# The third token group of batch 0 gets its second product as seven block products

## The chip, the cores and the metric

The kernel runs on one core of one Trainium2 chip. TensorE (PE in the profile) multiplies matrices, with weight loads shown as a unit of their own (PEld); VectorE (DVE), ScalarE (ACT) and GpSimd (POOL) work element by element; the SP queue and the POOL queue issue the DMAs. The metric is the device time of one execution in microseconds (us). The kernel before takes 362.45 us, the median of 3 runs (362.01 to 362.58).

## The reference

Attention over 4 batches of 768 tokens with 8 heads of 64, each token seeing 4 sink tokens and a window of 128, and behind it a dense mixture of 4 experts over the 3072 tokens:

```python
keep = is_sink | in_window
a = softmax(where(keep, scale * q @ k.T, -1e9))
x = (a @ v)                       # per batch [768, 8 * 64], together [3072, 512]
p = domain_probs / (domain_probs.sum(-1, keepdims=True) + 1e-09)
for e in range(E):                # 4 experts, w1 [512, 1024], w2 [1024, 512]
    h = np.maximum(x @ w1[e], 0.0)
    out += p[:, e:e + 1] * (h @ w2[e])
```

## The kernel before, in words

Tokens are taken in groups of 256; (b, g) is group g (0 to 2) of batch b (0 to 3). For each group and each expert e there is a *unit* (b, g, e): its first product `x @ w1[e]` with ReLU, kept in a tile H. There are at most 6 tiles H at a time (`NH = 6`); three more come free near the end.

**First products.** A *slow* unit is 32 products of 256 columns (line 1055). A *fast* unit multiplies 2 by 2 blocks with seven block products (`UNITS`, names P1 to P7), 56 products of 128 columns (line 1142), for which DVE forms sums of tokens (line 1111) and, once per expert, sums of the weights (`weight_form1`, lines 374 to 380), and for which ACT and DVE copy and add partial blocks (lines 1188, 1195, 1201, 1210). `START[e]` is the first (b, g) from which expert e is fast.

**Second products, batch 0.** Batch 0 has plain second products (`emit_second`): for each unit and each half s of the group 8 products of 512 columns (line 1394), then one DVE instruction that multiplies by the token's gate and adds to the output tile (lines 1404 and 1406). ReLU of batch 0 is done without the gate, on ACT or DVE, whichever is free (lines 1068, 1070, 1161, 1163). Each output half is stored through SP (line 1412).

**Second products, batches 1 to 3.** Here the gate is multiplied in with the ReLU, on DVE alone (`scalar_tensor_tensor`, lines 1079 and 1175), and the second product of a group is seven block products in the order `CHAIN = ("P1", "P2", "P6", "P5", "P7", "P3", "P4")` (`emit_product`). Since the gate is already in H, all four experts are summed in one PSUM bank: each block product is 4 experts times 4 products of 256 columns (line 1316). DVE forms four sums per unit of H for it (`chore`, lines 1260 and 1239) in two tiles S, and three or four sums of w2 per expert (`weight_form`, lines 338 to 344). A block's result goes out by a copy on ACT (line 1366; P1 also seeds the other bank, line 1348) or an addition on DVE (lines 1354 and 1359). `PAIRS` lists the groups done so: nine, all of batches 1 to 3. A tile H is held until its part of P4, the last.

Three facts tie batch 0 to the first of these groups. The tiles S lie in the buffers of the outputs of batch 0's groups 0 and 1, so that the sums of the first pair wait until these are stored. The sums of w2 of expert 3 lie in three buffers (`spare_rows`) that are left over once the six q and k tiles of batch 1 have been turned by DMA transposes on SP (line 243). And no block product is emitted while a plain second product is still due (`product_ready`).

**Order.** Everything is in one program order that a planner in the kernel writes: it keeps a modelled clock per engine, and at each step takes, among the instructions of TensorE that are ready, the one with the lowest priority number (attention steps, first products, block products, plain second products). Evictions wait in a list with a slack each (`GATE`, `MASK`, `FORM`, `TOKEN`), and go to ACT or DVE by it. If nothing is ready, it issues products of zeros (line 554). The constants at the top (lines 60 to 90) set priorities, slacks and the points at which the attention of the next batch begins (`LEAD`, in parts of the work done). The loads that POOL issues have a fixed order: after the attention of batch 0 it asks for w1 of expert 3, then for the rows of q, k and v of batch 1, and then for w2 of expert 3 (line 319). The gates per token are written to DRAM (line 438) and read back as one broadcast tile per unit (line 454), five at a time.

Of the kernel before, what the change touches and what calls it, by code (L numbers as in the profile page):

```python
# [16 lines left out]
def kernel(  # L17
# [14 lines left out]
    B, H, S, D = q.shape  # L32
    NSINK = int(n_sink)
    WIN = int(window)
    E, Dm, F = moe_w1.shape
    Ntok, Dout = out.shape

    P = 128
# [8 lines left out]
    NDB = Dm // P  # L47
    NFB = F // P
# [3 lines left out]
    G = 2 * P  # L52
    NG = S // G
# [6 lines left out]
    NGATE = 5  # L60
    START = {0: (0, 2), 1: (0, 2), 2: (0, 0), 3: (2, 1)}
    MIX = 4
    SHARE_OF = (0.98, 0.90, 1.01)
    LEAD = (0.92, 0.94)
    DUE = 0
    LOW_PRODUCT = 2.005
    LOW_SECOND = 2.7
    HIGH_PRODUCT = 1
    EARLY = 0.01
    MASK = 2500  # L70
    GATE = 3000
    GATE0 = 500
    FORM = 9000
    TOKEN = 5000
    MARGIN = 1000
    HOLD = 0
    FULL = 7
    STEP0 = 0.3
    READY = 40
    WIDE = 2  # L80
    OPEN = 2.6
    SOON = 21000
    ROWS1 = 1500
    ONACT = 1
    ONE = 2
    PAIR = 1
    BEHIND = 1500
    CHORES = 2
    OWN = 2
    BIASED = 1  # L90
    FAST = tuple(START)
# [292 lines left out]
    used, formed = set(), {}  # L384
    left = [NG] * E

# [54 lines left out]
    gate_sb = {}  # L441
# [474 lines left out]
    QF = NFB // 2  # L916
    PAIRS = [(b, g) for b in range(1, B) for g in range(NG)]
    CHAIN = ("P1", "P2", "P6", "P5", "P7", "P3", "P4")
# [3 lines left out]
    class Mixture:  # L922


        def __init__(self):
            self.early = {g: list(range(E)) for g in range(NG)}
            self.open = []
            self.units = []
            for b, g in PAIRS:
                fast = [e for e in range(E) if self.is_fast(b, g, e)]  # L930
                slow = [e for e in range(E) if e not in fast]
                while fast or slow:
                    for x in (fast, slow):
                        if x:
                            self.units.append((b, g, x.pop(0)))
# [28 lines left out]
        def opened(self, b, g, e):  # L964
# [9 lines left out]
            def complete(at):  # L974
                self.H_at[b, g, e] = at
                self.finished.add((b, g, e))
                if b:
                    self.waiting.append((b, g, e))
                    load_gates()
# [20 lines left out]
        def firsts(self):  # L1000

            early = sum(map(len, self.early.values()))
            zero = sum(u["unit"][0] == 0 for u in self.open)
            n = len(self.open)
# [8 lines left out]
            if n < WIDE and early:  # L1013
                at, g = self.next_early()
                yield at, (OPEN if n else 2), ("early", g)
            if n < WIDE and self.units and early <= MIX and self.room() and not (early + zero and self.live >= NH - 1):
                yield self.unit_ready(*self.units[0], False), (OPEN if n else 2) - EARLY, ("unit",)

        def emit_first(self, what, ready):
# [15 lines left out]
            b, g, e = u["unit"]  # L1035
            if j in (0, "P1") and (b, e) == (0, E - 1) and not gate_sb:
                load_gates()
            u["left"].remove(j)
            if not u["left"]:
                self.open.remove(u)  # L1040
                left1[e] -= 1
                if b == 0:
                    self.second += [(g, s, e) for s in range(2)]
# [20 lines left out]
            part = self.H_part[b, g, e]  # L1064
            if b == 0:
                def run(engine):
# [20 lines left out]
        def tokens(self):  # L1087

            pairs = [x for x in [(0, g) for g in range(NG)] + PAIRS if any(self.is_fast(*x, e) for e in FAST)]
            n = len(self.T)  # L1090
# [28 lines left out]
        def emit_fast(self, u, m, ready):  # L1119
# [37 lines left out]
            def gated(dst, src, half_, ready, slack, slot=None, then=None):  # L1157
                if b == 0:
                    def relu(engine):
# [59 lines left out]
        def chore(self):  # L1219
# [25 lines left out]
            if any(x[:2] < (b, g) and x[2] == "P5" for x in self.products) or any(x[:2] < (b, g) for x in self.last):  # L1245
                return False
            if (b, g) == PAIRS[0] and (len(self.stored) < 2 * NG or self.stored[-1] > t["pe"] + 500):
                return False
# [30 lines left out]
        def product_ready(self):  # L1279
# [8 lines left out]
            if m == "P1" and self.piece == E - 1 and acc_free[1 - bank] > 1e11:  # L1288
                at = 1e12
            if self.second or any(u["unit"][0] == 0 for u in self.open) or any(self.early.values()):  # L1290
                return 1e12
# [135 lines left out]
    att = Attention(0)  # L1427
    work = [E * NG * 2 * NFB * NDB * G - sum(mix.is_fast(0, g, e) for g in range(NG) for e in FAST) * NFB * P] + [NG * E * NFB * G * (NDB + 7 / 4) - sum(mix.is_fast(b, g, e) for g in range(NG) for e in FAST) * NFB * P for b in range(1, B)]
    ahead, upto, loaded, wide = 0, 0.0, 0, 0
# [22 lines left out]
    while mix.more() or att.more():  # L1452
# [5 lines left out]
        if not att.more() and not loaded:  # L1458
            loaded = 1
            gates_by_row()  # L1460
            turns += [(1, tb) for tb in range(NQB)]
            loads.append((load_w1, 3))
            for tb in range(NQB):
                loads.append((load_nat, 1, tb))
                if tb % 2:
                    loads += [(load_v, 1, (tb - 1,)), (load_v, 1, (tb,))]
            loads.append((load_w2, 3))
        x = next((x for x in loads if load_ready(x) < now + 1500), None)
# [39 lines left out]
        if soonest > 1e11:  # L1508
            if loads:
                x = loads.pop(0)  # L1510
                x[0](*x[1:])
            else:
                turn_nat(*turns.pop(0))
            continue
# [46 lines left out]
```

## Time and profile before

| | |
|---|---|
| median of 3 runs | 362.45 us |
| the profiled execution | 362.36 us, span 360.7 us |
| granted TensorE clock, mean | 0.999 |
| PE busy | 354.0 us (98%) |
| DVE busy | 299.2 us (83%) |
| ACT busy | 165.6 us (46%) |
| POOL busy | 71.3 us (20%) |
| line 1394, plain second products | 192 products |
| line 1316, block products | 1008 products |
| line 1142, fast first products | 2072 products |
| line 1055, slow first products | 352 products |

An engine's busy time is the time in which at least one of its instructions runs. For PE the ends are modelled, and products overlap: the row of line 1394 gives 379 ns for one, but eight in a row start 216 ns apart. The pace (starts of neighbours, or the length of a long run divided by its number) is what a product costs. The times run from the start of the span; the profiled execution took 1.7 us more than its span.

### The profile page before, as it was taken

The page shows a single profiled execution, that of the slowest core. Times are in us where ns is not written, and L with a number is a line of the kernel's source. Part 1 is how long each engine was busy: PE and PEld are TensorE (multiplying, and loading weights), DVE is VectorE, ACT ScalarE, POOL GpSimd, SP SyncE. Part 2 cuts the span into 40 slices and gives each one's busy share as a digit, 9 for nine tenths or more (in the row PEclk, how much of TensorE's full clock was granted, in tenths as well). Part 3 has the DMA queues.
Part 4 walks back from the last instruction along what each step waited for, and adds up shares of the span by engine and source line. Part 5 has one row for each costly group of instructions (what it writes and reads, how often), then busy time and mean ns, then how long its engine had stood idle before and what let it go on. Part 6 is the DMA issues. An engine that isn't in the chain of part 4 may idle for free.

```text
span 360.7 us, 10596 instructions
## 1 busy us (share of the span) xinstructions
PE 354.0 (98%) x4436; PEld 297.8 (83%) x4436; DVE 299.2 (83%) x671; ACT 165.6 (46%) x419; POOL 71.3 (20%) x92
## 2 busy tenths in 40 slices
PE   8899999999999999999999999999999999999996
PEld 3585767766668878898899899899999999999985
DVE  6775989896588989789879989969999898897850
ACT  5764734479483475464454365544213312213210
POOL 8936116400624307010610000000000000000000
PEclk9999999999999999999999999999999999999999
DMA  9999999999998999528998212122011011100011
GB/s 165 167 183 193 211 210 163 127 148 214 164 96 146 162 199 128 72 49 97 137 168 127 60 64 53 19 75 61 22 54 59 25 52 47 31 33 29 2 59 58
DMA packets 117291, 37.25 MB, mean 103 GB/s; under 512 B 100612, under 2 KB 112740, under 8 KB 117244
## 3 DMA queue, kind: packets, MB, share of 16 engines
q0 software_dynamic: 77520, 17.31, 54.4%
q1 hardware_dynamic: 38668, 18.75, 26.6%
q8 instruction: 34, 0.56, 0.6%
q10 hardware_dynamic: 1056, 0.52, 0.5%
q14 instruction: 13, 0.11, 0.1%
HBM read 40.45 MB, written 6.34 MB: 130 GB/s over the span
## 4 chain that ended last, share of the span: by engine, by line
PE 88%; DVE 6%; ACT 2%; DMA 1%; issue 1%; POOL 1%; ACTq 0%; DVEq 0%
PE cps L1142 31%; PE acc L1316 29%; PE acc L1394 11%; PE hps L1055 10%; PE od L747 3%; PE sps L681 3%; DVE H L1175 2%; DMA vx<-in_v_dram 1%; ACT aT L706 1%; PE od L740 1%; DVE S L1260 1%; PE tx L805 1%; DVE onat L777 1%; DVE H L1210 1%; DVE osb L1404 0%
## 5 line engine op out<-in xcount | busy, mean ns | idle before, releaser
L1142 PEld LDWEIGHTS <-w 128*128 128x128 bf16 x1184 | 73.6, 98 | 4.2 <-issue 1.3
L1316 PEld LDWEIGHTS <-H 128*128 128x128 bf16 x600 | 56.1, 98 | 6.1 <-issue 0.5
L706 ACT ACTIVATE aT<-sps 128x512 bf16<-128x512 f32 (+1 forms) x96 | 47.0, 571 | 16.2 <-PE sps L681 16.1
L1175 DVE SCALAR_TENSOR_TENSOR H<-cps,gates 128x512 bf16<-128x512 f32 x78 | 52.5, 681 | 0.8
L1142 PEld LDWEIGHTS <-vf 128*128 128x128 bf16 x768 | 47.0, 98 | 1.9 <-issue 0.3
L1316 PE MATMUL acc<-w,H 128*128 128x256 bf16 x360 | 47.5, 273 | 0.0
L1394 PE MATMUL acc<-w,H 128*128 128x512 bf16 x192 | 45.3, 379 | 0.0
L1142 PE MATMUL cps<-T,w 128*128 128x128 bf16 x592 | 45.0, 219 | 0.1
L1142 PE MATMUL cps<-xT,w 128*128 128x128 bf16 x592 | 44.7, 219 | 0.0
L1055 PE MATMUL hps<-xT,w 128*128 128x256 bf16 x352 | 43.6, 273 | 0.0
L786 ACT ACTIVATE onat<-od,R 128x64 bf16<-128x64 f32 x144 | 33.0, 330 | 19.2 <-DVE R L774 18.7
L1188 ACT COPY cps<-cps 128x512 f32<-128x512 f32 x37 | 21.4, 578 | 41.6 <-PE cps L1142 38.0
L1142 PE MATMUL cps<-T,vf 128*128 128x128 bf16 x512 | 37.4, 219 | 0.0
L1055 PEld LDWEIGHTS <-w 128*128 128x128 bf16 x352 | 33.0, 98 | 4.5 <-issue 0.6
L1394 PEld LDWEIGHTS <-H 128*128 128x128 bf16 x192 | 17.7, 98 | 18.1 <-issue 0.5
L296 POOL DMA_DIRECT2D vx<-in_v_dram x24 | 21.5, 911 | 53.8 <-PE od L747 40.9
L1316 PEld LDWEIGHTS <-S 128*128 128x128 bf16 x288 | 26.8, 98 | 3.3 <-issue 0.7
L1195 DVE TENSOR_TENSOR cps<-H,cps 128x512 f32<-128x512 f32 x31 | 21.4, 691 | 8.2 <-PE cps L1142 6.9
L1366 ACT COPY osb<-acc 128x256 f32<-128x256 f32 x28 | 10.5, 375 | 37.9 <-PE acc L1316 37.9
L700 DVE TENSOR_TENSOR aT<-aT,mask 128x1024 bf16<-128x1024 bf16 (+1 forms) x36 | 22.8, 638 | 3.3 <-ACT aT L706 3.1
L1210 DVE TENSOR_TENSOR H<-H,cps 128x512 f32<-128x512 f32 x31 | 21.2, 682 | 4.8 <-PE cps L1142 4.5
L1316 PE MATMUL acc<-wf,H 128*128 128x256 bf16 x176 | 23.8, 273 | 0.0
(129 smaller groups left out, 553.0 us busy)
## 6 DMA issues: line engine op xcount, KB each, us to landing
w<-in_moe_w_dram POOLq DMA_DIRECT2D x7, 1024.0 KB, 14.9
out_dram<-osb SPq DMA_DIRECT2D x19, 256.0 KB
gates<-gate_rows SPq DMA_DIRECT2D x36, 128.0 KB
vx<-in_v_dram POOLq DMA_DIRECT2D x24, 128.0 KB, 6.3
qkn<-in_q_dram POOLq DMA_DIRECT2D x22, 128.0 KB, 8.1
qkn<-in_k_dram POOLq DMA_DIRECT2D x22, 128.0 KB, 8.1
w<-in_moe_w_dram POOLq DMA_DIRECT2D x2, 512.0 KB, 8.6
out_dram<-aT SPq DMA_DIRECT2D x4, 256.0 KB
```

The costliest lines, as they stand in the source:

```text
L296: nc.gpsimd.dma_start(out=vx[tb][:, :, 0:D], in_=v[b, :, tb * P:(tb + 1) * P, :].rearrange("h p d -> p h d"),)
L700: nc.vector.tensor_mul(a, a, m[:, None, :].to_broadcast([P, 2, w]))
L706: nc.scalar.activation(out=a[:, ph], in_=sps[ph][:, 0:w], func=AF.Exp, scale=scale)
L786: nc.scalar.mul(o[:, qi, hp, ph * D:(ph + 1) * D], od[:, qi, ph, 0:D], R[:, qi, ph])
L1055: nc.tensor.matmul(h[:, i].rearrange("p (q n) -> p q n", q=2), lhsT=w1_sb[e][:, db, fb * P:(fb + 1) * P], rhs=xT[b, g][:, :, db], start=(i ...
L1142: nc.tensor.matmul(y[:, f], lhsT=A[:, d, f * P:(f + 1) * P], rhs=T[:, d], start=(m in ("P1", "P5") and f == 0 and d == 0), stop=(d == 1), ...
L1175: nc.vector.scalar_tensor_tensor(out=dst, in0=src, scalar=0.0, in1=gate, op0=ALU.max, op1=ALU.mult)
L1188: nc.scalar.copy(out=tiles["Y"], in_=y)
L1195: nc.vector.tensor_add(tiles["V"], c5, tiles["X"])
L1210: nc.vector.tensor_add(c5, c5, y)
L1316: nc.tensor.matmul(x, lhsT=self.operand(b, g, e, m)[:, f], rhs=forms[e][m][:, f], start=(k == 0 and f == 0 and m in (("P1", "P5", "P2") if ...
L1394: nc.tensor.matmul(op, lhsT=H[:, fb // QF, fb % QF, s], rhs=w2_sb[e][:, fb, :], start=(fb == 0), stop=(fb == NFB - 1),)
```

## The change

The third group of batch 0, (0, 2), leaves the plain second products and joins the pairs: `NEARLY = 2` is the number of groups of batch 0 that stay plain, and `PAIRS` has ten groups. With it, H of (0, 2) is gated at the ReLU on DVE, its gates are loaded, its tiles S are formed and its four H are held until P4. Its units are taken from the list `units` (with the rule that they open only after the attention of batch 0), all four one after the other in the order of the experts.

The load of w2 of expert 3 goes from the end of the list to the place ahead of the rows of batch 1's third tile (`W2AT = 2`); the first gates are loaded right after they are written. `START` makes expert 0 slow at (0, 2) and expert 3 fast from (2, 0) on. If nothing is ready and a store of batch 0 is still under way, the planner lets its clock pass without an instruction. Most of the constants of the order have new values.

```diff
-    START = {0: (0, 2), 1: (0, 2), 2: (0, 0), 3: (2, 1)}
-    MIX = 4
-    SHARE_OF = (0.98, 0.90, 1.01)
-    LEAD = (0.92, 0.94)
-    DUE = 0
-    LOW_PRODUCT = 2.005
+    START = {0: (1, 0), 1: (0, 2), 2: (0, 0), 3: (2, 0)}
+    MIX = 6
+    SHARE_OF = (0.91, 0.78, 1.08)
+    LEAD = (1.01, 0.90)
+    DUE = 1.5
+    LOW_PRODUCT = 2.7
     LOW_SECOND = 2.7
-    HIGH_PRODUCT = 1
-    EARLY = 0.01
-    MASK = 2500
-    GATE = 3000
+    HIGH_PRODUCT = 1.9
+    EARLY = -0.01
+    MASK = 4000
+    GATE = 1500
     GATE0 = 500
-    FORM = 9000
+    FORM = 6000
     TOKEN = 5000
-    MARGIN = 1000
+    MARGIN = 500
 ...
-    STEP0 = 0.3
+    STEP0 = 0.01
 ...
-    OPEN = 2.6
+    OPEN = 2.2
     SOON = 21000
+    NEARLY = 2
+    W2AT = 2
 ...
-    CHORES = 2
+    CHORES = 3
 ...
-    left = [NG] * E
+    left = [NEARLY] * E
 ...
-    PAIRS = [(b, g) for b in range(1, B) for g in range(NG)]
+    PAIRS = [(b, g) for b in range(B) for g in range(NG) if (b, g) >= (0, NEARLY)]
 ...
-            self.early = {g: list(range(E)) for g in range(NG)}
+            self.early = {g: list(range(E)) for g in range(NEARLY)}
 ...
                 slow = [e for e in range(E) if e not in fast]
+                if b == 0:
+                    fast, slow = list(range(E)), []
 ...
-                if b:
+                if (b, g) >= PAIRS[0]:
                     self.waiting.append((b, g, e))
                     load_gates()
 ...
-            if n < WIDE and self.units and early <= MIX and self.room() and not (early + zero and self.live >= NH - 1):
+            if n < WIDE and self.units and (self.units[0][0] or loaded) and early <= MIX and self.room() and not (early + zero and self.live >= NH - 1):
 ...
-            if j in (0, "P1") and (b, e) == (0, E - 1) and not gate_sb:
-                load_gates()
 ...
-                if b == 0:
+                if (b, g) < PAIRS[0]:
                     self.second += [(g, s, e) for s in range(2)]
 ...
-            if (b, g) == PAIRS[0] and (len(self.stored) < 2 * NG or self.stored[-1] > t["pe"] + 500):
+            if (b, g) == PAIRS[0] and (len(self.stored) < 2 * NEARLY or self.stored[-1] > t["pe"] + 500):
 ...
             gates_by_row()
+            load_gates()
             turns += [(1, tb) for tb in range(NQB)]
             loads.append((load_w1, 3))
             for tb in range(NQB):
+                if tb == W2AT:
+                    loads.append((load_w2, 3))
                 loads.append((load_nat, 1, tb))
                 if tb % 2:
                     loads += [(load_v, 1, (tb - 1,)), (load_v, 1, (tb,))]
-            loads.append((load_w2, 3))
 ...
         if soonest > 1e11:
-            if loads:
+            if mix.stored and mix.stored[-1] > now:
+                t["pe"] += 200
+            elif loads:
```

More of the change, by code (lines that the diff above doesn't have):

```diff
@@ L1002, in firsts @@
             early = sum(map(len, self.early.values()))
-            zero = sum(u["unit"][0] == 0 for u in self.open)
+            zero = sum(u["unit"] < PAIRS[0] for u in self.open)
             n = len(self.open)
@@ L1064, in emit_first @@
             part = self.H_part[b, g, e]
-            if b == 0:
+            if (b, g) < PAIRS[0]:
                 def run(engine):
@@ L1087, in tokens @@
         def tokens(self):
-            pairs = [x for x in [(0, g) for g in range(NG)] + PAIRS if any(self.is_fast(*x, e) for e in FAST)]
+            pairs = [x for x in [(0, g) for g in range(NEARLY)] + PAIRS if any(self.is_fast(*x, e) for e in FAST)]
             n = len(self.T)
@@ L1157, in gated @@
             def gated(dst, src, half_, ready, slack, slot=None, then=None):
-                if b == 0:
+                if (b, g) < PAIRS[0]:
                     def relu(engine):
@@ L1289, in product_ready @@
                 at = 1e12
-            if self.second or any(u["unit"][0] == 0 for u in self.open) or any(self.early.values()):
+            if self.second or any(u["unit"] < PAIRS[0] for u in self.open) or any(self.early.values()):
                 return 1e12
@@ L1427 @@
     att = Attention(0)
-    work = [E * NG * 2 * NFB * NDB * G - sum(mix.is_fast(0, g, e) for g in range(NG) for e in FAST) * NFB * P] + [NG * E * NFB * G * (NDB + 7 / 4) - sum(mix.is_fast(b, g, e) for g in range(NG) for e in FAST) * NFB * P for b in range(1, B)]
+    work = [sum(NFB * NDB * G * (1 if (b, g) < START[e] else 7 / 8) + NFB * NDB * G * (1 if (b, g) < PAIRS[0] else 7 / 8) for g in range(NG) for e in range(E)) for b in range(B)]
     ahead, upto, loaded, wide = 0, 0.0, 0, 0
```

## The prediction

> **What bounds the kernel now.** I read the page's first part, then the chain that ended last by line, then the groups of the lines that change, then the busy time by stretch around the place of the change.
>
> ```profile
> PE 354.0 (98%) x4436; PEld 297.8 (83%) x4436; DVE 299.2 (83%) x671; ACT 165.6 (46%) x419; POOL 71.3 (20%) x92
> ...
> PE 88%; DVE 6%; ACT 2%; DMA 1%; issue 1%; POOL 1%; ACTq 0%; DVEq 0%
> ```
>
> TensorE is busy for 98% of the span and is 88% of the chain. As busy PE can hide short holes (one product's modelled end lies up to 160 ns behind the next one's start), I took the starts of neighbouring products in the timeline against their pace: from 25 us to the end the holes add up to about 2.4 us, and to another 5.4 us at 58 changes between attention scores, which use half the array's rows, and other work, about 93 ns each. Behind 40 us only three single holes are over 0.2 us: 0.42 us at 126.2 us (a mask on DVE), 0.28 us at 297.5 us and 0.21 us at 124.7 us. So behind the start-up the time is the sum of the products. What a product costs is read from runs of equal products in the chain:
>
> ```profile
> 48.76 1.75 PE hps L1055 x16
> 50.51 0.89 PE cps L1142 x16
> 59.32 1.73 PE acc L1394 x8
> 139.47 1.75 PE acc L1316 x16
> ```
>
> That is 0.109 us for a product of line 1055, 0.056 us for one of line 1142, 0.216 us for one of line 1394 (512 columns) and 0.109 us for one of line 1316 (256 columns). The groups give the instructions that change on the other engines, with the mean duration of one behind the busy time:
>
> ```profile
> L1142 PEld LDWEIGHTS <-w 128*128 128x128 bf16 x1184 | 73.6, 98 | 4.2 <-issue 1.3
> L1175 DVE SCALAR_TENSOR_TENSOR H<-cps,gates 128x512 bf16<-128x512 f32 x78 | 52.5, 681 | 0.8
> ...
> L1068 ACT ACTIVATE H<-hps 128x512 bf16<-128x512 f32 x23 | 13.7, 597 | 14.4 <-PE hps L1055 14.2
> L1406 DVE SCALAR_TENSOR_TENSOR osb<-acc,scale_t,osb 128x512 f32<-128x512 f32 x18 | 13.5, 748 | 8.7 <-PE acc L1394 8.5
> ...
> L1260 DVE TENSOR_TENSOR S<-H 128x512 bf16<-128x512 bf16 x30 | 12.0, 417 | 0.8 <-PE acc L1316 0.6
> ```
>
> Last, stretches of 20 us around the change (columns: PE, PEld, DVE, ACT, POOL busy, granted clock, DMA) and three rows of POOL and SP and two of DVE from the timeline:
>
> ```profile
> 65.00:85.00 20.00, 20.00 (x215) 12.93 (x213) 15.60 (x33) 12.60 (x37) 3.06 (x4) 1.00 1.73 152
> 85.00:105.00 20.00, 20.00 (x236) 14.59 (x234) 14.66 (x34) 14.13 (x40) 8.06 (x10) 1.00 1.60 174
> 105.00:125.00 20.00, 19.95 (x263) 16.92 (x262) 16.83 (x33) 8.60 (x23) 7.89 (x9) 1.00 1.29 130
> 125.00:145.00 20.00, 19.74 (x227) 15.25 (x227) 18.45 (x42) 13.79 (x40) 6.32 (x8) 1.00 1.54 164
> ```
> ```profile
> 46.92 0.87 POOL L296 DMA_DIRECT2D vx<-in_v_dram  x1 [3.75 <-DMA w<-in_moe_w_dram]
> 51.98 0.87 POOL L231 DMA_DIRECT2D qkn<-in_q_dram  x1 [4.18 <-DMA w<-in_moe_w_dram]
> ...
> 73.23 0.88 POOL L319 DMA_DIRECT2D w<-in_moe_w_dram  x1 [1.97 <-DMA vx<-in_v_dram]
> ```
> ```profile
> 82.05 5.12 SPq L243 DMA_TRANSPOSE qkT<-qkn  x1
> ```
> ```profile
> 100.04 0.68 DVE L338 TENSOR_TENSOR qkn<-w 128x1024 bf16<-128x1024 bf16 x1
> ...
> 105.53 0.69 DVE L342 TENSOR_TENSOR qkn<-w,qkn 128x1024 bf16<-128x1024 bf16 x1
> ```
>
> DVE has 4.4, 5.3, 3.2 and 1.6 us to spare in the four stretches. POOL's load issues stand 5.06 us apart where each waits for one 1024 KB weight load (46.92, 51.98). w2 of expert 3 was asked for at 73.23 us, the last row tile of batch 1 was turned by 87.2 us, and expert 3's sums of w2 came from 100.0 to 106 us.
>
> **The change part by part.** The sum is made against the profiled execution, 362.36 us (span 360.7, 1.7 outside it), 0.09 us below the median.
>
> *Products.* 4 experts x 2 halves x 8 = 64 products of line 1394 go: 64 x 0.216 = 13.84 us. 7 x 4 x 4 = 112 of line 1316 come: 112 x 0.109 = 12.25 us. Both lie on the path, as PE never rests there: -1.6 us. `START` makes one unit slow (32 x 0.109 - 56 x 0.056 = +0.4 us) and another fast (-0.4 us): nothing.
>
> *Weight loads.* Each product has its own, so 48 more at 98 ns, 4.7 us of PEld. In the row of line 1142, 1184 loads of 98 ns would be 116 us one by one and take 73.6 us: loads overlap each other and the products, and at line 1316 the pace, 109 ns, is longer than a load. I cost them at nothing. The Trainium skill (Perfetto Trace Analysis, Identifying the Most-Contended Engine) holds product busy time to be a poor measure of how near the limit one is and wants the weight loads' busy share instead; that share, 83% here, goes up with this change, by which it would be no gain. The rival it makes is priced below.
>
> *DVE.* 8 gate-and-add instructions go (8 x 0.75 = 6.0 us). 16 ReLUs of (0, 2), of which by batch 0's split (36 of 48 on ACT) some 4 were on DVE at 0.6 to 0.7, become 16 gated ones on DVE: +10.9 - 2.6 = +8.3 us. 16 sums of H come: 16 x 0.417 = 6.7 us; 2 output additions, 0.8 us. Together +9.8 us by durations, less back to back, since neighbours overlap (two sums in 0.76 us, four gated ReLUs in 2.48 us): about +8 us. ACT loses 12 ReLUs (12 x 0.60) and gains five copies (5 x 0.37): -5.3 us. Most of it falls between 65 and 125 us, where DVE has 12.9 us to spare. DVE would be 92% busy there. In the same view the stretch of 260 to 280 us has 19.32 of 20 us of DVE and 19.98 of PE, so the cover holds at 97% too. Cost nothing; if the 8 us fall into 40 us with 8.5 to spare, a backlog of up to 3 us that PE waits for.
>
> *w2 of expert 3 earlier.* One POOL issue of 0.88 us is moved past the issues of four row tiles (eight, 0.9 us each) and of four v tiles, and all of these land some 5.1 us later. In the SP queue the turn of the last rows ends about 92 us in place of 87.2, and behind it stand the turn of xT (1, 0) and the stores; attention of batch 1's groups 1 and 2 is due later. The first gates (five issues of 0.3 to 0.8 us) no longer stand between two turns, where they took 77.8 to 82.0 us: up to 4 us back. The cover is PE's other work, below. Between -0.3 (the hole at 126.2 us goes) and +4.5 us (below); I take 0, since the cover is longer than the delay.
>
> *What is late next: the chain into (0, 2).* Its block products need all 16 plain second products, the stores, the sums S, and from P6 on expert 3's sums of w2. These need the last turn (92 us) and three DVE instructions of 0.68 us; I put them at 95 to 97 us. The stock of PE work at 45 us that needs none of this, by the counts of each line's products before 45 us: second products 128 - 36 done = 92 x 0.216 = 19.9 us; slow first products 256 - 104 = 152 x 0.109 = 16.6; fast 224 x 0.056 = 12.5; attention of batch 1's groups 0 and 1, some 4; P1 and P2, 32 x 0.109 = 3.5. That is 56.5 us and lasts to about 101 us, 4 us longer than needed. H is no bar once groups 0 and 1 are through: four tiles for (0, 2), two for (1, 0).
>
> *New order.* Changed constants move everything; the trace prices neither end directly. It can gain at most the holes, 2.4 us, and some of the 5.4 us of changes (each attention pair split or joined is 0.19 us, so -0.8 to +0.8 us for four); in the first 20 us PE is idle 2.9 us, waiting for data, -1 to +1. It can lose by a plan whose clocks the chip does not keep: the nearest rows are the holes just named, so +2.4 us for as many again. I take 0, as before's order lost little.
>
> *Sum:* 362.36 - 1.6 = 360.8 us, 360.85 against the median; I say 360.8.
>
> **Rivals.** *The gain is eaten by the order* (no change): the 1.6 us come back as holes and changes between attention and other work, 15 to 20 places of 0.09 us. For it: 58 changes stand now, and the priorities of attention steps move. Against: nothing in the trace makes their number grow. 362.4 us.
>
> *DVE becomes the bound between 85 and 125 us* (slower, the other side): gated ReLUs can't go to ACT, their PSUM banks come free late, and first products wait for a bank. For it: DVE stood on the chain from 119.1 to 126.6 us already, and 125 to 145 us is 92% busy. Against: 65 to 105 us has 9.7 us free. It decides where DVE would need more than 97% of 40 us; 3 us of backlog give 362.4 + 3 - 1.6 = 363.8 us.
>
> *PE runs dry before P6* (slower): expert 3's sums come where they came before, 105.5 us, while the stock ends at 101. 4.5 - 1.6 = +2.9, 365.3 us. Products of zeros at line 554 would show after 80 us. Against: their first condition, w2 landed (87.8 us before), comes some 20 us earlier, and units of (1, 0) fill in from about 98 us.
>
> *Weight loads set the pace* (slower): 48 x 98 ns = 4.7 us more, 367.1 us. Against it is the overlap of line 1142.
>
> **How the numbers follow.** Forecast 0.58; eaten 0.13; DVE 0.14; dry 0.13; weight loads 0.02. A difference of 0.2% (0.7 us) is about what can be told. Faster is the forecast alone, 0.58; within 0.2% "eaten", 0.13; slower the last three, 0.29. The forecast's own range is 359.7 (1.1 us of the holes gone as well) to 361.7. The whole range reaches up through "eaten" and DVE with another 0.8 us of changes, 364.6, and leaves out "dry" and "weight loads" and a little below.
>
> **What the next profile would show.** Right: line 1394 with 128, line 1316 with 1120 products at the same paces, PE busy 1.6 us shorter at 98% or more, gated ReLUs 16 more, weight load of line 319 issued near 52 us, expert 3's sums of w2 before 98 us, no line 554 behind 20 us. Wrong: holes of PE ended by DVE between 85 and 125 us, zeros' products, or more than 60 changes into attention scores. A start-up longer by a microsecond or a later batch whose attention begins late would make the number wrong with the mechanism right.

## The result, and the profile after

The kernel after the change takes 366.09 us, the median of 6 runs (365.46 to 366.61), against 362.14 us (361.97 to 362.58, 6 runs) for the kernel before: a ratio of 1.0106, with a 95% interval of 1.0092 to 1.012. It is 1.1% slower, where 0.4% faster was forecast. The profiled execution of after took 366.61 us with a span of 364.9 us, 4.2 us more than the span of before.

The page of after: busy time, the clock by fortieths of the span, and the chain by engine and then by line.

```profile
PE 352.8 (97%) x4476; PEld 302.6 (83%) x4484; DVE 303.9 (83%) x690; ACT 162.7 (45%) x415; POOL 71.5 (20%) x92
...
PEclk9999998999999999999999999999999999999999
...
PE 87%; DMA 5%; DVE 4%; POOL 2%; ACT 1%; issue 1%; SPq 0%; DVEq 0%; ACTq 0%
PE acc L1318 34%; PE cps L1144 32%; PE hps L1057 9%; PE acc L1396 5%; PE sps L683 3%; PE od L749 2%; DMA w<-in_moe_w_dram 2%; DMA gates<-gate_rows 2%; DMA gate_rows<-scratch 1%; POOL qkn L233 1%; PE od L742 1%; POOL vx L298 1%; DVE aT L717 0%; DVE onat L779 0%; ACT aT L708 0%
```

PE is busy 1.2 us less than before although the span is longer, so its time went into standing still. (The lines have moved by two: 1394 is now 1396, 1316 is 1318, 1142 is 1144, 1055 is 1057.) Two names are new on the chain: `gate_rows`, the gates written to DRAM, and `gates`, the gates read back. The clock has one lower slice, the seventh, 55 to 64 us. The busy time by stretches of 20 us (columns: sum, PE, PEld, DVE, ACT, POOL, clock, DMA share, GB/s) shows the place. Before, 40 to 60 us:

```profile
40.00:60.00 20.00, 20.00 (x209) 15.05 (x206) 18.37 (x36) 10.02 (x19) 5.25 (x6) 1.00 1.46 197
```

After, the same stretch and the two behind it:

```profile
40.00:60.00 20.00, 16.13 (x125) 11.19 (x123) 13.03 (x28) 5.11 (x10) 3.39 (x4) 0.98 1.34 210
60.00:80.00 20.00, 19.31 (x221) 15.25 (x222) 18.27 (x30) 7.82 (x14) 8.50 (x11) 0.94 1.78 168
80.00:100.00 20.00, 19.79 (x210) 13.20 (x211) 15.34 (x34) 12.96 (x40) 5.35 (x8) 1.00 1.48 145
```

PE lacks 3.9 us of work between 40 and 60 us, and runs at a clock of 0.94 in the next 20. The stretch of 85 to 125 us, where the prediction looked for danger, is not it. The chain of after through that place (start, duration, what) names what it waits for:

```profile
44.86 1.07 DVE scratch L436
46.92 5.42 DMA gate_rows<-scratch
52.39 6.15 DMA gates<-gate_rows
58.64 0.70 DVE H L1081
59.38 3.52 PE hps L1057 x16
```

The waits of after between 38 and 85 us (total, times, longest) agree:

```profile
DVE H L1081 <- DMA gates<-gate_rows: 6.7, 1, 6.7
...
PE hps L1057 <- DVE H L1081: 3.8, 1, 3.8
```

So: the gates are formed on DVE until 45.9 us, their write to DRAM lands 5.42 us after the step before it, their read back another 6.15 us later. The first gated ReLU of unit (0, 2), line 1081, stands at the head of DVE's queue all that time, as DVE's timeline in after shows:

```profile
51.29 0.69 DVE L346 TENSOR_TENSOR w<-w 128x1024 bf16<-128x1024 bf16 x1
58.64 0.69 DVE L1081 SCALAR_TENSOR_TENSOR H<-hps,gates 128x512 bf16<-128x512 f32 x1 [6.66 <-DMA gates<-gate_rows]
```

None of the instructions that the program has behind it on DVE starts before it, so for 6.66 us DVE does nothing at all, and PE's timeline in after shows what that costs:

```profile
53.73 1.89 PE L1396 MATMUL acc<-w,H 128*128 128x512 bf16 x8
59.38 3.52 PE L1057 MATMUL hps<-xT,w 128*128 128x256 bf16 x16 [3.76 <-DVE H L1081]
...
66.83 0.61 PE L1144 MATMUL cps<-T,w 128*128 128x128 bf16 x8 [0.59 <-DVE cps L1197]
```

PE runs out of free PSUM banks at 55.2 us and starts its next product at 59.38: a hole of 3.9 us by the starts. The 16 products behind it take 3.52 us, where 16 of this line took 1.75 us in the kernel before: half the pace, +1.8 us. At 66.0 us DVE's backlog costs another 0.75 us. Together 6.4 us.

The balance by starts of products, beyond 25 us: the holes are 9.1 us in after, less 1.7 us for eight records of line 1396 that the trace lacks (8 x 0.216), so 7.4, against 2.4 us before: +5.0. Changes between attention and other work are 60 or 61, by how they are counted, in place of 58: about +0.2. Products: -1.6. The sum, +3.6 us, is what the start of the last product moved by, from 357.27 to 360.83 us. The other 0.65 us of the 4.2 come behind the last product; an experiment below finds them.

In before the gates were written at the same moment (46.05 us against 45.96), so the same slow trip lay under other work. There the read was asked for at 77.77 us and the first gated ReLU came at 110.61 us:

```profile
77.77 4.18 SPq L454 DMA_DIRECT2D gates<-gate_rows  x5
...
110.61 0.69 DVE L1175 SCALAR_TENSOR_TENSOR H<-cps,gates 128x512 bf16<-128x512 f32 x1
```

### The profile page after: what moved, and what is told of

The parts are those of the page before. It is cut to its first block, busy times and chain, and to the rows that moved or that the text cites. A ratio compares the mean times of both kernels' runs of the same rounds, so it can differ in the third digit from the quotient of the medians.

```text
span 364.9 us, 10705 instructions
## 1 busy us (share of the span) xinstructions
PE 352.8 (97%) x4476; PEld 302.6 (83%) x4484; DVE 303.9 (83%) x690; ACT 162.7 (45%) x415; POOL 71.5 (20%) x92
## 4 chain that ended last, share of the span: by engine, by line
PE 87%; DMA 5%; DVE 4%; POOL 2%; ACT 1%; issue 1%; SPq 0%; DVEq 0%; ACTq 0%
PE acc L1318 34%; PE cps L1144 32%; PE hps L1057 9%; PE acc L1396 5%; PE sps L683 3%; PE od L749 2%; DMA w<-in_moe_w_dram 2%; DMA gates<-gate_rows 2%; DMA gate_rows<-scratch 1%; POOL qkn L233 1%; PE od L742 1%; POOL vx L298 1%; DVE aT L717 0%; DVE onat L779 0%; ACT aT L708 0%
## 5 line engine op out<-in xcount | busy, mean ns | idle before, releaser
L1318 PEld LDWEIGHTS <-H 128*128 128x128 bf16 x700 | 65.0, 98 | 8.0 <-issue 1.5
L1177 DVE SCALAR_TENSOR_TENSOR H<-cps,gates 128x512 bf16<-128x512 f32 x90 | 60.7, 684 | 0.1
L1318 PE MATMUL acc<-w,H 128*128 128x256 bf16 x420 | 55.4, 273 | 0.0
L1057 PE MATMUL hps<-xT,w 128*128 128x256 bf16 x352 | 44.9, 278 | 3.9 <-DVE H L1081 3.8
L1144 PEld LDWEIGHTS <-vf 128*128 128x128 bf16 x744 | 45.6, 98 | 1.2 <-issue 0.5
L1144 PE MATMUL cps<-xT,w 128*128 128x128 bf16 x592 | 43.7, 219 | 0.0
L1368 ACT COPY osb<-acc 128x256 f32<-128x256 f32 x36 | 13.6, 377 | 50.5 <-PE acc L1318 50.5
L1318 PEld LDWEIGHTS <-S 128*128 128x128 bf16 x320 | 30.4, 98 | 3.4 <-issue 0.2
L1396 PE MATMUL acc<-w,H 128*128 128x512 bf16 x120 | 29.3, 379 | 0.6 <-issue 0.3
L1318 PE MATMUL acc<-wf,H 128*128 128x256 bf16 x208 | 29.3, 273 | 0.0
L1396 PEld LDWEIGHTS <-H 128*128 128x128 bf16 x128 | 12.1, 98 | 12.1 <-issue 0.2
```

The source lines that it names most:

```text
L1057: nc.tensor.matmul(h[:, i].rearrange("p (q n) -> p q n", q=2), lhsT=w1_sb[e][:, db, fb * P:(fb + 1) * P], rhs=xT[b, g][:, :, db], start=(i ...
L1144: nc.tensor.matmul(y[:, f], lhsT=A[:, d, f * P:(f + 1) * P], rhs=T[:, d], start=(m in ("P1", "P5") and f == 0 and d == 0), stop=(d == 1), ...
L1177: nc.vector.scalar_tensor_tensor(out=dst, in0=src, scalar=0.0, in1=gate, op0=ALU.max, op1=ALU.mult)
L1318: nc.tensor.matmul(x, lhsT=self.operand(b, g, e, m)[:, f], rhs=forms[e][m][:, f], start=(k == 0 and f == 0 and m in (("P1", "P5", "P2") if ...
L1396: nc.tensor.matmul(op, lhsT=H[:, fb // QF, fb % QF, s], rhs=w2_sb[e][:, fb, :], start=(fb == 0), stop=(fb == NFB - 1),)
```

## The experiments

The theory (*gates*): the change gave the gates a first reader at about 52 us, and the 11.6 us of their two DMAs are not hidden any more; products, weight loads and DVE's extra work are as forecast. Rivals: the new order or the earlier w2 costs the time by itself (*order*, *w2*); or the loss is mostly the half clock behind the hole (*clock*); or PE was short of one PSUM bank (*bank*). Each run was compared with runs of before on the same chip, whose medians were 362.66, 362.34 and 362.32 us in the three groups of runs.

### The gates early, all else in place (gates_early)

```diff
+        if now > 28000 and not gate_sb: kept = dict(t); gates_by_row(); load_gates(); t.update(kept)
 ...
-            gates_by_row()
-            load_gates()
+            dve(1800, 0.0)
+            [sp(takes=300) for _ in range(NGATE)]
```

The gates are formed, written and read from 28 us on; the planner's clocks are put back as they were, so that the order of every other instruction stays that of after: in the traces PE's weight loads and all instructions of ACT come in the same order in both kernels, and on DVE only the four that form the gates stand elsewhere.

> The changed kernel with the gates of all tokens formed, written to DRAM and the first five tiles read back while attention of batch 0 still runs (near 28 us in place of 43 us); the planner's clocks are left as they were, so that every other instruction keeps its place. Theory 'gates late' (DVE stands 6.66 us before the first gated ReLU of group (0, 2) until its gate tile lands at 58.5 us, PE stands 3.9 us behind it, runs 16 products at half the pace, 1.8 us, and loses another 0.75 us to DVE's backlog at 66 us): all of this goes, 366.1 - 6.4 = 359.7, at most 361 us; no hole over 0.5 us between 50 and 70 us. Rival 'DVE or the stock of work is the bound there anyway': the hole moves by a few us and the time stays above 363 us. Rival 'the order costs it': 365 to 366 us.

Measured: 362.35 us (361.36 to 362.69, 10 runs), 0.9984 of before (0.9973 to 0.9995). That is 3.7 us less than after's median, from another group of runs whose before was 0.5 us higher. The profiled execution is the slowest of the ten. The hole at 55 us and the half pace behind it are gone. What is left above the forecast is a new hole, in the waits of this kernel's PE:

```profile
PE acc L1396 <- DVE osb L1406: 1.4, 1, 1.4
```

The four DVE instructions of the gates, of 1.07 us the longest, now stand ahead of an eviction at 32.5 us. By starts the hole is 1.5 us, and the last product starts at 356.9 us, 0.4 us earlier than in before. *Gates* holds: with this one wait gone the whole loss against before is given back, though not yet the forecast gain.

### The gates in an earlier gap of DVE (gates_gap)

```diff
-                    gates()
+                    kept = dict(t); gates_by_row(); load_gates(); t.update(kept); gates()
 ...
-            gates_by_row()
-            load_gates()
+            dve(1800, 0.0)
+            [sp(takes=300) for _ in range(NGATE)]
```

The same, but put into the program order ahead of the first plain second product; SP issues the writes at 28.5 us.

> As gates_early, but the four DVE instructions that form the gates stand where DVE was idle for 2.4 us (25.9 to 28.3 us, ahead of the reading of the token gates by line 909); every other instruction keeps its place. gates_early still had a hole of 1.5 us in PE at 32.5 us, which ended with an output sum that DVE made late because of these four. Theory 'gates late, and the products themselves gain 1.6 us': that hole shrinks to 0.6 us or less and the time is 362.35 - 1 = 361.3 us or below, faster than the kernel before by 0.2 to 0.5%. Rival 'the block products gain nothing net': 362.3 us again, with holes in other places.

Measured: 361.63 us (361.2 to 362.12, 10 runs), 0.9978 of before (0.9967 to 0.9988). Its page and its stretches:

```profile
PE 352.2 (98%) x4484; PEld 302.4 (84%) x4484; DVE 303.3 (84%) x690; ACT 162.8 (45%) x415; POOL 72.3 (20%) x92
```
```profile
40.00:60.00 20.00, 20.00 (x185) 15.04 (x184) 17.21 (x34) 6.41 (x13) 3.47 (x4) 1.00 1.31 211
60.00:80.00 20.00, 20.00 (x209) 14.46 (x205) 15.79 (x30) 8.98 (x17) 9.80 (x12) 1.00 1.83 170
80.00:100.00 20.00, 18.93 (x238) 13.50 (x238) 16.23 (x36) 14.75 (x47) 6.14 (x8) 1.00 1.58 166
```

PE is full from 40 to 80 us at a clock of 1.00. The holes by starts are 2.25 us against 2.36 in before, so this kernel is the change as the prediction imagined it, and its last product starts at 355.5 us, 1.8 us earlier than in before; the sum of the products was -1.6. One large hole is left, which PE's timeline puts down to the late rows of batch 1:

```profile
87.39 0.29 PE L644 MATMUL sinks<-qkT,ksd 128*32 128x256 bf16 x4 [1.07 <-DMA qkT<-qkn]
```

Of the 1.8 us, the profiled execution keeps 1.1 us (361.23 against 362.36), the median of the runs 0.7, and 361.63 us lies 0.3 us above what was expected of this run. The profiled execution was the second fastest of its ten; why the others lie up to 0.9 us above it was not settled.

### The hole filled with products (hole_filled)

```diff
+    def fill_hole(slot, n):
+        if n == 19:
+            i = min((i for i in range(6) if i != slot), key=lambda i: ring[i])
+            x = psum.tile([P, 2 * G], FP32, name="zero", tag=f"r{i}", bufs=1)
+            for _ in range(34):
+                nc.tensor.matmul(x[:, 0:G], lhsT=zeros[:, 0:P], rhs=zeros[:, 0:G], start=True, stop=True)
 ...
-            slot = pick(False)
+            slot = pick(False); slows.append(e); fill_hole(slot, len(slows))
```

After, with 34 products of zeros where PE stood, into a bank that is not read. This keeps the clock up and leaves the order of the other instructions as it was.

> The changed kernel with 34 products of zeros of 256 columns (34 x 0.109 = 3.7 us) put into PE's order just where it stands, into a PSUM bank that is not in use; nothing else changes, the hole stays. If the slow products after the hole (16 in 3.52 us) are the clock that was taken back in the hole, they take 1.75 us and the time is 366.1 - 1.8 = 364.3 us (a little more if the zeros end late). If they are slow for another reason, 366.1 us.

Measured: 365.96 us (365.88 to 366.37, 4 runs), 1.0096 of before (1.0081 to 1.0111). PE's timeline, and behind it the first gated ReLU in DVE's:

```profile
55.06 3.88 PE L564 MATMUL zero<-lent 128*128 128x256 bf16 x34
58.80 1.03 PE L1065 MATMUL hps<-xT,w 128*128 128x256 bf16 x8
60.66 1.03 PE L1065 MATMUL hps<-xT,w 128*128 128x256 bf16 x8 [0.82 <-DVE H L1089]
...
66.25 0.61 PE L1152 MATMUL cps<-T,w 128*128 128x128 bf16 x8 [0.75 <-DVE cps L1205]
```
```profile
58.06 0.69 DVE L1089 SCALAR_TENSOR_TENSOR H<-hps,gates 128x512 bf16<-128x512 f32 x1 [6.48 <-DMA gates<-gate_rows]
```

The clock is 1.00 throughout and the products behind the hole run at full pace, and yet the time falls by only 0.1 us (0.7 us when each kernel is set against the before of its own group of runs). In the profiled execution the last product starts 0.6 us earlier than in after, and so does the first gated ReLU (58.06 us against 58.64). PE reaches the next bank sooner and there waits for DVE, which has 6.48 us to make up: holes of 0.99, 0.47 and 0.92 us between 59 and 66 us. *Clock* falls: most of the half pace was time in which PE would have waited anyway. On the mechanism, the Trainium skill (TensorE: Matmul & The Clock Gate, What's actually happening) says that about 3.4 us of idleness bring the array to half its clock; the hole of 3.9 us followed by 16 products at half pace agrees. Holes of 1.92 us (order_alone) and 2.10 us (other_bank) were followed by half pace as well, so here less idleness than that sufficed. What it cost in after, though, was 0.1 to 0.7 us and not the 1.8 us read off the products.

### Another bank for the same products (other_bank)

```diff
-            slot = pick(False)
+            slows.append(e); slot = pick(len(slows) in (19, 20, 21, 22))
```

The products that stood in after get a pair of banks that DVE's waiting instruction doesn't hold.

> The changed kernel, where the slow first products number 19 to 22 go to PSUM banks that have been free since 40 us, in place of the banks that wait for the gated ReLU; a few DVE and PE instructions behind change places. If PE's wait for the bank is what costs, PE goes on at 55.5 us, the hole of 3.9 us is gone or short and the time falls by 3 us or more, to 363 us. If DVE's 6.7 us of standing are what costs, PE meets a hole of DVE's backlog a little later, and the time falls by less than 1 us, to no less than 365 us.

Measured: 366.81 us (366.1 to 367.84, 4 runs), 1.012 of before (1.0102 to 1.0139). PE's timeline:

```profile
56.29 1.91 PE L1057 MATMUL hps<-xT,w 128*128 128x256 bf16 x16
...
62.07 0.91 PE L1144 MATMUL cps<-T,vf 128*128 128x128 bf16 x8 [1.93 <-ACT cps L1190]
...
65.17 1.86 PE L1144 MATMUL cps<-T,vf 128*128 128x128 bf16 x16 [1.34 <-DVE H L1081]
```

There is no hole at 55 us any more. PE goes on to 59 us and then stands 0.60, 2.10 and 1.60 us. From 62 to 69 us the granted clock is 0.52, and the products of line 1144 run at half pace there (16 in 1.86 us, where before has 0.89), which adds some 2.4 us by the starts. *Bank* falls as the cause of the loss: the work that PE does early, it lacks later, as DVE did nothing for 5.96 us here. How much this kernel would lose without the half clock is not shown.

### The units held back (units_later)

```diff
-            if n < WIDE and self.units and (self.units[0][0] or loaded) and early <= MIX and ...
+            if n < WIDE and self.units and (self.units[0][0] or loaded and t["pe"] > gates_in[0]) and early <= MIX and ...
 ...
             load_gates()
+            gates_in[0] = now + 14000
```

The units of (0, 2) open only 14 us after the gates are asked for, by the planner's clock: the wait is removed from the other side, and the order is planned anew.

> The changed kernel, gates where they are, but the units of group (0, 2) open no sooner than 14 us after the gates are formed, so that the planner finds other work (the plan behind is a new one). If the stock of other work is large enough at 50 us, no hole stands before 65 us and the time is 361 to 363 us. If the stock is short there, PE runs zeros or waits, and the time is 364 to 367 us.

Measured: 365.78 us (364.64 to 366.04, 4 runs), 1.0084 of before (1.0067 to 1.01). No instruction waits for the gates. Instead, PE's waits show

```profile
PE cps L1145 <- DVE cps L1198: 3.1, 2, 2.6
```

In place of the gated ReLUs the planner put eight sums of weights on DVE between 52.3 and 58.7 us, and an addition that PE's next fast products need came behind them; by starts the hole is 2.8 us at 56.6 us. Removing the wait is not enough if what the planner puts in its place stands ahead of the same engine. This run does not speak against *gates*; it shows a second way to lose 3 us at the same place.

### The order alone (order_alone)

```diff
-    NEARLY = 2
+    NEARLY = 3
```

After's constants, its place of w2 and its START, but all three groups of batch 0 with plain second products and nine pairs, as in before.

> The changed kernel with NEARLY = 3: all three groups of batch 0 keep plain second products, but w2 of expert 3 is asked for early and all constants of the order and START are the new ones. Theory 'gates late': no gated ReLU before about 100 us, so no hole near 55 us; 362.4 us, give or take 1 us. Rival 'the new order is worse by itself': 364 us or more, with holes or more changes to attention scores in other places.

Measured: 364.82 us (364.37 to 367.03, 5 runs), 1.0062 of before (1.0045 to 1.0079). PE's longest wait is

```profile
PE sinks L644 <- DMA qkT<-qkn: 1.9, 1, 1.9
```

The turned rows of batch 1 come late at 86.4 us; the seven products behind them run 0.21 us longer each, another 0.6 us is lost at 134.8 us, and there are 65 changes into and out of attention in place of 58. This execution is the slowest of the five, 367.03 us at a granted clock of 0.995; the other four ran at 1.000, so the seven slow products are no part of the median. By the medians, the new order and the earlier w2, without the change that they were fitted to, cost 2.2 us. `START` was not changed alone.

### The earlier w2 alone (w2_alone)

```diff
             for tb in range(NQB):
+                if tb == 2:
+                    loads.append((load_w2, 3))
 ...
-            loads.append((load_w2, 3))
```

This is the kernel before, with expert 3's w2 asked for ahead of batch 1's third row tile.

> The kernel before with only the load of w2 of expert 3 moved ahead of the third row tile of batch 1 (the planner orders the rest anew by its own rules). Theory 'gates late': nothing to do with it, 362.4 us within 1 us. Rival 'rows 5 us later starve attention of batch 1': 364 to 367 us with a hole between 80 and 110 us.

Measured: 364.05 us (363.73 to 364.98, 4 runs), 1.0045 of before (1.0028 to 1.0062): +1.4 us. Its holes by starts are 3.8 us in place of 2.4, the largest at 93.8, 144.7 and 150.1 us (0.61, 0.41 and 0.36 us). Rows that land later are not free, as the prediction had it.

### Is the earlier w2 needed? (gap_w2last, gap_w2at4, gap_rows_first)

gap_w2last is gates_gap with w2 last, as in before, and a new plan:

```diff
-    W2AT = 2
+    W2AT = 9
 ...
+            loads.append((load_w2, 3))
```

> As gates_gap, but w2 of expert 3 is asked for last, as in the kernel before; the plan behind is a new one. If the early w2 is needed for the block products of (0, 2), since these wait for all plain second products: zeros or holes between 80 and 110 us and 363 to 368 us. If the early w2 only delays the rows of batch 1 (w2_alone was 1.4 us slower than the kernel before), it is the faster of the two, 360 to 361 us.

gap_w2at4 is gates_gap with `W2AT = 4`, w2 ahead of the fifth tile, also planned anew:

> As gates_gap with W2AT = 4: the load of w2 of expert 3 one pair of row tiles later, known to the planner, which writes a new plan. If the lateness of the rows is all that is left, 360 to 361 us; if a new plan has holes of its own, as units_later, order_alone and gap_w2last had, 363 to 366 us.

gap_rows_first is gates_gap with the DMA of w2 alone moved behind the rows of tile 3 of batch 1, and the planner's clocks and the rest of the order untouched:

```diff
+        qkn_free.append(1e12); (b, tb) == (1, 3) and nc.gpsimd.dma_start(out=w2_sb[E - 1], in_=moe_w2[E - 1].rearrange("(fb p) d -> p fb d", p=P))
 ...
-        nc.gpsimd.dma_start(out=w2_sb[e], in_=moe_w2[e].rearrange("(fb p) d -> p fb d", p=P))
+        if e < E - 1: nc.gpsimd.dma_start(out=w2_sb[e], in_=moe_w2[e].rearrange("(fb p) d -> p fb d", p=P))
```

> As gates_gap, with nothing moved but one DMA in POOL's queue: w2 of expert 3 goes behind the q and k rows of the third and fourth tile of batch 1 in place of ahead of them. gates_gap had a hole of 1.1 us at 86.1 us where attention waits for the turn of the fourth tile. If the early w2 made these rows late, the hole goes, 361.6 - 1 = 360.6 us. If w2 then lands too late for the plain second products that need it from 78 us on, a hole of up to 3 us stands near 78 us in its place.

Measured: 366.08 us (365.38 to 367.47), 367.75 us (364.87 to 368.45) and 368.12 us (367.97 to 368.96), 4 runs each; 1.0103 (1.0081 to 1.0124), 1.0123 (1.0091 to 1.0154) and 1.0164 (1.0151 to 1.0177) of before. PE's waits in gap_w2last:

```profile
PE acc L1318 <- DVE S L1262: 2.0, 1, 2.0
PE acc L1396 <- DMA w<-in_moe_w_dram: 1.6, 1, 1.6
```

PE's wait in gap_w2at4:

```profile
PE acc L1396 <- DMA w<-in_moe_w_dram: 5.5, 1, 5.5
```

The transfer of w2 in gap_rows_first, in its chain, and PE's wait for it:

```profile
62.48 21.55 DMA w<-in_moe_w_dram
```
```profile
PE acc L1396 <- DMA w<-in_moe_w_dram: 4.1, 1, 4.1
```

All three lose 4 to 7 us to gates_gap. Expert 3's plain second products of groups 0 and 1 need this w2, and moved behind rows it lands 21.55 us after the step before it, at 84.0 us; in gates_gap it was asked for 8.3 us earlier, at 54.20 us, and landed after 16.7 us. So the earlier w2 costs by itself (w2_alone), and with ten pairs all three later places measured are slower still. In gap_w2last the plan is new as well, and its longest wait is for a sum S, so that not all of its loss is w2's. In gap_w2at4 the plan was made anew and still has PE wait 5.5 us for this load: it seems that here, as with the gates, the planner's clock gives a load a shorter landing than it has among other loads.

### The end of the kernel (gap_split, gap_both)

From the issue of the last store to the end of the span takes 360.7 - 357.97 = 2.7 us in before and 364.9 - 361.53 = 3.4 us in after. In gates_gap, from which gap_split differs, it is 359.5 - 356.16 = 3.4 us. The last store in before, in after, in gates_gap and in gap_split (span 360.0), from each one's SP timeline:

```profile
357.97 0.33 SPq L1308 DMA_DIRECT2D out_dram<-osb  x1
```
```profile
361.53 0.33 SPq L1310 DMA_DIRECT2D out_dram<-osb  x1
```
```profile
356.16 0.33 SPq L1310 DMA_DIRECT2D out_dram<-osb  x1
```
```profile
357.36 0.33 SPq L1310 DMA_DIRECT2D out_dram<-osb  x1
```

The last store lands about 1.4 us behind its issue in both kernels. At the end SP waits for the semaphores of its DMAs one after another, in an order that does not follow the stores: the one of the last store is last but one in before, and in after five waits are left behind it, some 0.7 us. The semaphore that the last store gets, and so its place in that order, changes with the number of DMAs that SP has issued. gap_split is gates_gap with five DMAs more on SP, one store of pair (2, 0) in six pieces:

```diff
-                    nc.sync.dma_start(out=out[r:r + P, :], in_=o[0])
+                    [nc.sync.dma_start(out=out[r + i:r + j, :], in_=o[0][i:j]) for i, j in (((0, 24), (24, 48), (48, 72), (72, 96), (96, 112), (112, 128)) if (b, g) == (2, 0) else ((0, P),))]
```

> As gates_gap, with one output store of group (2, 0) (256 KB, in the middle of the run) issued as six pieces, so that SP issues five DMAs more. In all kernels with the third group of batch 0 among the pairs the time from the last product's start to the end of the span is 4.0 to 4.1 us, in the kernels without 3.3 to 3.4: SP waits for the semaphores of its DMAs in a fixed order at the end, and the last store's stands fourth there, with five left behind it, where before it stands last but one. Five DMAs more move the last store to the end of that order. If this is the cause, the time from the last product to the end is 3.4 us again and the time falls by 0.6 us. If it is not, 4.0 us and 361.6 us.

Measured: 361.5 us (360.56 to 361.83, 7 runs), 0.9968 of before (0.9956 to 0.9981). From the last issue to the end of the span are now 360.0 - 357.36 = 2.6 us, so the lost 0.7 us are back there. In the time the step from gates_gap (0.9978) is 0.1%, and the two intervals overlap, so the stores' part of the gain is shown in the trace and not in the times. This is the fastest version found, 0.3% ahead of before and 1.3% ahead of after (361.5 against 366.09).

gap_both joins gap_split with the late w2 of gap_rows_first.

> gap_rows_first and gap_split together: 361.6 - 1 - 0.6 = 360.0 us if both hold, 0.6% below the kernel before.

Measured: 366.79 us (362.43 to 369.25, 7 runs), 1.0091 of before (1.0057 to 1.0125). Its runs are spread over 6.8 us, and the granted clock goes with them: 0.999 in the fastest, 0.989 to 0.995 in the others (in gap_w2at4 1.000 in the fastest, 0.991 in the slowest). The profiled one has a hole of 5.15 us at 78.9 us, at the same place as in gap_rows_first; that the spread comes from the landing of w2, and from the half clock behind the hole, fits this, but the other runs left no trace, and it is not shown.

## Why the prediction was wrong

**The step that failed** is the price of the moved gates. Under "w2 of expert 3 earlier" the prediction counted the gates only as an issue that "no longer stand[s] between two turns", worth "up to 4 us back", and under "what is late next" the chain into (0, 2) listed second products, stores, sums S, w2 and H, but not the gates. It did not ask who reads the gates first in the new order. In before that is a ReLU at 110.6 us; in after it is one at about 52 us, 6 us after the gates are formed, behind two DMAs that depend on each other and take 5.42 and 6.15 us. The price in the runs: gates_early, which changes this alone, is 3.7 us faster than after, and gates_gap 4.5 us (differences of medians; the befores of their groups of runs lay 0.5 and 0.2 us above that of after).

**DVE as the bound.** That rival named the engine, at 85 to 125 us and by the amount of its work. The engine was right, the place (52 to 66 us) and the mechanism wrong: it was not too much work but an instruction at the head of the queue that nothing behind it passed. It needed no 97% of busy time; DVE was 65% busy from 40 to 60 us. Where the rival looked, from 85 to 125 us, DVE was busy for 37.17 of 40 us (24.93 of the last 25) and PE for 39.77, so that high a load cost next to nothing. The rival's 3 us come from no row: 8 us of work into 8.5 us to spare leave no backlog by themselves.

**Products, -1.6 us: right.** Line 1318 has 1120 products and the eight of line 1396 missing from the trace make 128, at unchanged paces; gates_gap, with holes as in before, starts its last product 1.8 us earlier.

**Weight loads at nothing: right.** PEld grew from 297.8 to 302.4 us in gates_gap, as forecast (4.7), and its share from 83 to 84%, while the time fell by 0.2%. The Trainium skill (Perfetto Trace Analysis, Identifying the Most-Contended Engine) names the weight loads' busy share, together with the share of the peak rate of operations, as a measure of how close a kernel is to its limit. It does not say that a change that raises the share gains nothing; that was the prediction's reading, and the measurement decides against it.

**DVE, +8 us: mis-sized.** DVE grew by 4.7 us (299.2 to 303.9) and ACT shrank by 2.9 us (5.3 forecast). In after, the plain ReLUs of batch 0 on ACT are 27, 21 of line 1070 and 6 of line 1163, so of the 32 that are left only 5 are on DVE, where before 12 of 48 were: the planner gave back part of what the gated ones took. The groups of after for ACT's and DVE's terms:

```profile
L1070 ACT ACTIVATE H<-hps 128x512 bf16<-128x512 f32 x21 | 12.5, 597 | 14.4 <-PE hps L1057 14.2
```
```profile
L1177 DVE SCALAR_TENSOR_TENSOR H<-cps,gates 128x512 bf16<-128x512 f32 x90 | 60.7, 684 | 0.1
L1262 DVE TENSOR_TENSOR S<-H 128x512 bf16<-128x512 bf16 x35 | 14.5, 422 | 2.5 <-PE acc L1318 2.4
...
L1408 DVE SCALAR_TENSOR_TENSOR osb<-acc,scale_t,osb 128x512 f32<-128x512 f32 x12 | 9.0, 746 | 2.3 <-PE acc L1396 2.1
```

**The earlier w2 at 0: mis-sized.** Alone it measured +1.4 us, and gates_gap still has 1.1 us of it as a hole at 86 us, where the rows' last turn is late. The cover named, "PE's other work", was there in quantity, but attention was the next thing in the written order. The range (-0.3 to +4.5) held it.

**The new order at 0: mis-sized.** The order and w2 without the change cost 2.2 us (order_alone); less w2's 1.4 that leaves 0.8 us for the constants, as an estimate across two kernels. The larger finding is that each new plan with ten pairs measured here (units_later, gap_w2last, gap_w2at4) ended at 365.8 to 367.8 us, by waits that the plan did not hold.

**PE dry before P6: did not happen.** Expert 3's sums of w2 came from 90.3 us on in after and 83.8 in gates_gap, and no products of zeros were issued behind 20 us.

**Missed altogether:** the 0.65 us behind the last product. With it the forecast's -1.6 could at best have been about -1.0.

## What to carry to other kernels

When a step is moved forward, look for the first reader of everything that the step needs, and add up the whole chain of DMAs from where the data is formed, at the durations that the trace shows while the loads run; a value that was early for one reader can be late for a new one. An instruction that waits at the head of an engine's queue, as DVE's did here for 6.66 us, holds up all that stands behind it: before moving PSUM banks or filling holes, make what it waits for earlier. And a hole's length with the slow products behind it need not measure what closing it brings; the engine that was late must have caught up as well.

## What the runs showed of the hardware

Small DMAs took long while the 1024 KB weight loads were under way: two stores of 24 KB each 5.42 us on the chain, a load of 128 KB, the first of five issued one behind the other, 6.15 us, where a store of 256 KB landed some 1.4 us after its issue at the quiet end. The Trainium skill (DMA: Bandwidth & Descriptors, Anatomy of one DMA — SWDGE (gpsimd) path) gives a fit of about 2 us plus the bytes at 436 GB/s for one DMA, by which the load would be about 2.3 us (an estimate from that page, made for the other kind of queue); under this load the trace has 2.7 times that. The load of expert 3's w2, 1024 KB, took 21.55 us on the chain behind row loads (gap_rows_first) and 16.7 us ahead of them (gates_gap).

A hole of 3.9 us halved the pace of the next 16 products (3.52 us in place of 1.75). Behind the hole of 1.92 us in order_alone seven products ran at half pace too, and behind those of 2.10 and 1.60 us in other_bank 47 did; behind those of 0.99 us and less in hole_filled and the one of 1.07 us in gates_gap none did. It did not come each time: the other four executions of order_alone had a granted clock of 1.000.

The end of the span depended on how many DMAs SP had issued: 3.4 us behind the last issue in gates_gap, and 2.6 us with five DMAs more and the same last store (gap_split); 2.7 us in before.
